# The first warm-up of TensorE: five matmuls of 512 columns instead of eight

## The chip, the core and the metric

The kernel runs on one core of a Trainium2 chip. A core has a matrix engine (TensorE, "PE" in the profile, with its weight loads shown apart as "PEld"), a vector engine (VectorE, "DVE"), a scalar engine (ScalarE, "ACT"), a general engine (GpSimd, "POOL") and a queue engine (SyncE, "SP"). They run side by side and wait for each other through semaphores. The metric is the device time of one execution in microseconds.

## What is computed

The reference is attention with two kinds of heads, followed by a mixture of four experts that all see every token:

```python
# q, k, v: (4 batches, 8 heads, 768 tokens, 64)
scores = scale * q @ k.T
mask   = causal                                  # heads 0, 2, 6
         or causal & (sink of 4 | window of 64)  # heads 1, 3, 4, 5, 7
a   = softmax(where(mask, scores, -1e9))
x   = (a @ v) -> (3072 tokens, 512)
p   = domain_probs / (domain_probs.sum(-1) + 1e-9)   # (3072, 4)
out = sum over e of p[:, e] * (relu(x @ w1[e]) @ w2[e])   # w1: 512 x 1024, w2: 1024 x 512
```

## The kernel before

All instructions of all engines stand in an order written out by hand: each engine runs its own list in the order in which the program issues it, and each waits only where its data do.

The attention is cut into eight blocks (four batches, two halves of 384 tokens). Block 0, `attention(0, 0)`, is issued by itself at the start. The other seven are woven into the experts' matmuls by a plan of costs and due times. The experts' work takes the 24 tiles of 128 tokens in order: tiles 0 to 3 first (`plain_steps`), then pairs of tiles (`pair_steps`).

Only block 0 matters here, because the change stands right before it. Its parts on TensorE come in this order:

- `warm_up(ps_warm, 8, 512)` (called at L1461; the matmul is L446): matmuls of a tile of zeros, `warm`, which VectorE clears first (L431). They write a PSUM bank that nobody reads.
- `transposes(0)` (L574): q and k of heads 0 and 1 are turned by six f32 matmuls against an identity, three for q and three for k. q and k of this block come by their own DMAs, one for each head: eight for k on SP's queue (L409), the first four for q on ACT's queue and four on SP's (L422). The identity is made on POOL (masks.py).
- `scores(0)` (L676, with the mask added by L688). It begins with another `warm_up` of five matmuls of 128 columns (L446), which stands between the transposes and the first real matmul. That matmul waits for VectorE's copy of the keys out of PSUM into `kR` (L593).
- `transposes(1)` (heads 2 and 3), `scores(2)` with a `warm_up` of eight matmuls of 128 columns, then scores and values of the other heads mixed, with small warm-ups of 256 columns at five more places, and `transposes(2)` and `transposes(3)` between them. ScalarE takes the exponentials (L694) and the reciprocals of the sums (L822, L832).
- At the end the result is turned (L781) and scaled (L827) into `xT`, and the first experts' matmuls (L1050) read it, from 21.7 us on.

```python
    def warm_up(ps, n, cols):
        for _ in range(n):
            nc.tensor.matmul(
                out=ps[:, 0:cols], lhsT=warm[:, 0:P], rhs=warm[:, 0:cols],
                start=True, stop=True,
            )
```

Of the kernel before, what the change touches and what calls it, by code (L numbers as in the profile page):

```python
# [19 lines left out]
def kernel(  # L20
# [421 lines left out]
    ps_warm = pO.tile([P, DM], FP32, name="pO", bufs=2)  # L442
# [7 lines that stand above are left out]
# [1008 lines left out]


    nc.vector.memset(x_one[:, :, D:P], 0.0)  # L1460
    warm_up(ps_warm, 8, 512)  # L1461
    for ns in attention(0, 0):
        tick(ns)
    tick(LAG)
# [107 lines left out]
```

## Time and profile before

| what | value |
|---|---|
| median of 5 runs | 377.7 us (377.23 to 378.61) |
| profiled execution | 377.59 us, of which span 375.9 us |
| PE busy | 368.5 us, 98% of the span, 4128 matmuls |
| PEld / DVE / ACT / POOL busy | 83% / 72% / 61% / 30% |
| DMA | 39.24 MB, mean 104 GB/s |
| PE from 21.7 us to the end | 350.25 of 354.20 us busy |

The span is the time from the first to the last instruction of the program in the profiled execution; the device time holds some 1.7 us more around it. All starts below are counted from the span's start. Matmuls are pipelined: the length that the profile gives a matmul includes a tail that overlaps the next one, so the distance between two starts tells what a matmul really takes. "Idle before" in brackets is the time in which an engine had nothing to do before an instruction, with what ended the wait as far as the profile can tell from the semaphores; when an instruction waits for several, the last event before its start is named. The page's second part cuts the span into 40 slices, a digit for each: tenths of busy time, and for PEclk tenths of the full clock that TensorE was granted.

### The profile page before, as it was taken

Reading aid. Unit: us, or ns where it says so; the run is one execution under the profiler, and the core shown is the slowest. Engines: PE = TensorE matmul, PEld = TensorE weight load, DVE = VectorE, ACT = ScalarE, POOL = GpSimd, SP = SyncE. Lnnn points to the kernel's source line nnn. Section 1 sums busy time; section 2 is a strip of 40 time slices with the busy share of each in tenths; the row PEclk is TensorE's granted clock in tenths of the full one; section 3 lists DMA queues with packets and bytes.
Section 4 is the critical chain, followed back from the end, with each engine's and each line's share of the span. In section 5 each row is a group of like instructions: output and inputs, shape, how many; then the busy total and the mean of one; then the engine's idle time right before and its main releaser. Section 6 shows DMA issues by size and latency. Waiting matters only on the chain.

```text
span 375.9 us, 10100 instructions
## 1 busy us (share of the span) xinstructions
PE 368.5 (98%) x4128; PEld 311.2 (83%) x4128; DVE 271.5 (72%) x581; ACT 227.9 (61%) x475; POOL 112.6 (30%) x155
## 2 busy tenths in 40 slices
PE   8899999999999999999999999999999999999996
PEld 5755466668998988999989898998899998999995
DVE  7774768697787669868668858967768858559461
ACT  3863478547785785765776855784777361551630
POOL 8924673854057039115501650320000000000000
PEclk9999999999999999999999999999999999999999
DMA  8999999999699599998904991951220300300101
GB/s 157 157 203 208 192 188 193 172 171 151 103 109 153 91 98 123 159 114 63 198 4 64 170 157 25 126 121 12 72 68 3 114 2 0 114 2 22 37 2 57
DMA packets 123747, 39.24 MB, mean 104 GB/s; under 512 B 113728, under 2 KB 116356, under 8 KB 123700
## 3 DMA queue, kind: packets, MB, share of 16 engines
q0 software_dynamic: 85824, 19.01, 59.8%
q1 hardware_dynamic: 36276, 19.18, 22.9%
q8 instruction: 32, 0.52, 0.6%
q10 hardware_dynamic: 1600, 0.39, 0.5%
q14 instruction: 15, 0.12, 0.1%
HBM read 44.89 MB, written 6.34 MB: 136 GB/s over the span
## 4 chain that ended last, share of the span: by engine, by line
PE 95%; DVE 2%; ACT 2%; issue 0%
PE pO L1315 31%; PE pA L1179 25%; PE pO L1208 9%; PE pA L1050 7%; PE pO L1071 7%; PE pA L676 6%; PE pV L732 2%; PE pV L804 2%; PE pA L1208 2%; PE pO L446 1%; PE pA L574 1%; ACT es L694 1%; DVE xs L1135 1%; PE pA L1405 0%; ACT rc L822 0%; DVE xT L827 0%
## 5 line engine op out<-in xcount | busy, mean ns | idle before, releaser
L1315 PEld LDWEIGHTS <-hA 128*128 128x128 f16 x1104 | 104.9, 98 | 12.3
L1179 PE MATMUL pA<-xs,w1sb 128*128 128x256 f16 x864 | 109.3, 272 | 0.0
L1179 PEld LDWEIGHTS <-w1sb 128*128 128x128 f16 x864 | 80.7, 98 | 8.5
L1188 ACT ACTIVATE hA<-pA 128x512 f16<-128x512 f32 x108 | 64.4, 597 | 35.2 <-PE pA L1179 33.0
L1315 PE MATMUL pO<-w2sb,hA 128*128 128x256 f16 x640 | 76.7, 272 | 0.0
L694 ACT ACTIVATE es<-pA 128x384 f16<-128x384 f32 (+2 forms) x122 | 59.2, 512 | 26.7 <-PE pA L676 22.9
L306 POOL DMA_DIRECT2D vS<-in_v_dram x30 | 29.6, 986 | 110.0 <-PE pV L804 108.2
L1315 PE MATMUL pO<-tsb,hA 128*128 128x256 f16 x464 | 56.7, 272 | 0.0
L1135 DVE TENSOR_TENSOR xs<-xT,pB 128x1024 f16<-128x1024 f16 (+1 forms) x52 | 49.5, 970 | 1.4 <-DMA xT<-x_pair 1.4
L990 DVE TENSOR_TENSOR hA<-hA 128x1024 f16<-128x1024 f16 x60 | 39.7, 685 | 0.4
L1063 ACT ACTIVATE hA<-pA 128x384 f16<-128x384 f32 (+1 forms) x64 | 22.2, 385 | 19.4 <-PE pA L1050 19.2
L1050 PE MATMUL pA<-xT,w1sb 128*128 128x384 f16 (+1 forms) x256 | 31.1, 273 | 0.7 <-DVE xT L827 0.3
L1071 PE MATMUL pO<-w2sb,hA 128*128 128x512 f16 x128 | 30.7, 379 | 0.0
L1335 ACT COPY s<-pO 128x256 f32<-128x256 f32 x31 | 11.5, 372 | 27.7 <-PE pO L1315 21.9
L827 DVE TENSOR_TENSOR xT<-pV,rc 64x384 f16<-64x384 f32 x37 | 20.5, 555 | 10.3 <-ACT rc L832 7.8
L1050 PEld LDWEIGHTS <-w1sb 128*128 128x128 f16 x256 | 19.3, 98 | 9.8 <-issue 1.5
L1208 PEld LDWEIGHTS <-w1sb 128*128 128x128 f16 x416 | 26.3, 98 | 1.1 <-issue 0.2
L1225 DVE CUSTOM_DVE_ANT_0 hA<-pO,s 128x512 f16<-128x512 f32 x26 | 17.7, 689 | 12.5 <-PE pO L1208 8.8
L822 ACT ACTIVATE rc<-pV,eps 64x384 f32<-64x384 f32 x37 | 21.3, 575 | 6.5 <-PE pV L804 5.9
L698 DVE TENSOR_TENSOR es<-es,mS 128x384 f16<-128x384 f16 (+1 forms) x40 | 13.7, 344 | 15.0 <-ACT es L694 15.0
L676 PE MATMUL pA<-qT,kR 128*128 128x384 f16 (+2 forms) x120 | 23.1, 280 | 0.4 <-DVE kR L593 0.2
L1218 ACT COPY s<-pO 128x512 f32<-128x512 f32 x39 | 22.5, 586 | 1.4 <-PE pO L1208 1.2
(144 smaller groups left out, 487.6 us busy)
## 6 DMA issues: line engine op xcount, KB each, us to landing
pB<-p_rows SPq DMA_DIRECT2D x10, 512.0 KB
out_dram<-o SPq DMA_DIRECT2D x19, 256.0 KB
w1sb<-in_moe_w_dram POOLq DMA_DIRECT2D x8, 512.0 KB, 9.2
w2sb<-in_moe_w_dram POOLq DMA_DIRECT2D x4, 1024.0 KB, 12.3
vS<-in_v_dram POOLq DMA_DIRECT2D x30, 112.0 KB, 4.5
k_rows<-in_k_dram POOLq DMA_DIRECT2D x18, 128.0 KB, 5.0
q<-in_q_dram POOLq DMA_DIRECT2D x18, 128.0 KB, 6.9
vR<-in_v_dram POOLq DMA_DIRECT2D x24, 48.0 KB, 5.6
```

The costliest lines, as they stand in the source:

```text
L306: gp.dma_start(out=t[:, :, own_v(h)], in_=windows_of(v, b, h, c))
L676: nc.tensor.matmul(out=ps[:, o : o + nq], lhsT=key_tile(b, c, h, t), rhs=qTs[b, c][:, hp, q0 : q0 + nq], start=(n == 0 or not first), stop ...
L694: nc.scalar.activation(out=es[:, 0:cols], in_=ps[:, 0:cols], func=AF.Exp, scale=SC)
L990: nc.vector.tensor_tensor(out=out, in0=a, in1=b, op=ALU.subtract)
L1050: nc.tensor.matmul(out=pss[ft][:, 0:cols_n], lhsT=w1_tile(e, ct, ft), rhs=x[:, ct, :], start=(n == 0), stop=(n == DMP - 1),)
L1071: nc.tensor.matmul(out=ps_o, lhsT=hs[:, ft, j * P : (j + 1) * P], rhs=w2sb[:, e * FTP + ft, :], start=(ft == 0), stop=(ft == FTP - 1),)
L1135: nc.vector.tensor_tensor(out=o, in0=xin, in1=pb.to_broadcast([P, DMP, n, P]), op=ALU.mult)
L1179: nc.tensor.matmul(out=ps[:, f * PC : (f + 1) * PC], lhsT=w1_tile(e, ct, f0 + f), rhs=xs[:, ct, :], start=(ct == 0), stop=(ct == DMP - 1),)
L1188: nc.scalar.activation(out=blocks[:, b0 : b0 + 2, k0 : k0 + 2, :].rearrange("p t f x -> p f t x"), in_=ps.rearrange("p (f t x) -> p f t x" ...
L1208: nc.tensor.matmul(out=ps[:, f * P : (f + 1) * P], lhsT=w[:, ct, f * P : (f + 1) * P], rhs=a[:, ct, :], start=(first and f == 0 and ct == ...
L1218: nc.scalar.copy(out=kept[n], in_=ps)
L1315: nc.tensor.matmul(out=ps, lhsT=a[:, k, :], rhs=b(k), start=(first and k == 0), stop=(k == KT - 1), skip_group_check=not first,)
```

## The change

The number of matmuls in the first warm-up goes from eight to five. The width of 512 columns, the operands and the place stay.

```diff
     nc.vector.memset(x_one[:, :, D:P], 0.0)
-    warm_up(ps_warm, 8, 512)
+    warm_up(ps_warm, 5, 512)
     for ns in attention(0, 0):
         tick(ns)
     tick(LAG)
```

On TensorE three pairs of weight load and matmul (L446) fall out at the head of the list. The rest of that list, and the lists of the other engines, hold the same instructions in the same order.

## The prediction

> **What bounds the kernel now.** I read the page first: busy shares, granted clock, chain that ended last.
>
> ```profile
> PE 368.5 (98%) x4128; PEld 311.2 (83%) x4128; DVE 271.5 (72%) x581; ACT 227.9 (61%) x475; POOL 112.6 (30%) x155
> ...
> PEclk9999999999999999999999999999999999999999
> ...
> PE 95%; DVE 2%; ACT 2%; issue 0%
> ```
>
> TensorE (PE) is the bound, and no DMA stands in the chain. A microsecond that PE loses at the start comes out at the end, unless some wait after the place of the loss is ended by something that does not move with PE. The slices cannot show the start: 40 slices of 9.4 us are too coarse.
>
> Next, the timeline of PE and of its weight loads (PEld) from 1 to 10 us. Columns: start, length from the first start to the last end, engine and line, shapes, count, and in brackets the idle time before it and what ended it.
>
> ```profile
> 1.27 3.59 PE L446 MATMUL pO<-early 128*128 128x512 f16 x8 [1.27 <-DVE early L431]
> 3.80 0.15 PEld L446 LDWEIGHTS <-early 128*128 128x128 f16 x1 [0.28 <-issue]
> 4.55 1.19 PEld L574 LDWEIGHTS pA<-early,hA 128*128 128x128 f32 x6 [0.59 <-POOL early L466]
> 4.66 1.49 PE L574 MATMUL pA<-early,hA 128*128 128x128 f32 x6
> 5.94 0.74 PE L446 MATMUL pA<-early 128*128 128x128 f16 x5
> 6.79 0.61 PE L676 MATMUL pA<-qT,kR 128*128 128x128 f16 x2
> 7.19 0.32 PE L688 MATMUL pA<-early,ident 128*128 128x256 f16 x1
> 7.34 0.27 PE L676 MATMUL pA<-qT,kR 128*128 128x256 f16 x1
> 7.45 0.22 PE L688 MATMUL pA<-early,ident 128*128 128x128 f16 x1
> 7.51 0.82 PE L574 MATMUL pA<-early,hA 128*128 128x128 f32 x6
> 8.26 0.61 PE L446 MATMUL pA<-early 128*128 128x128 f16 x8
> 8.97 0.11 PEld L676 LDWEIGHTS <-kR 128*128 128x128 f16 x2 [0.29 <-DVE kR L593]
> 8.98 0.39 PE L676 MATMUL pA<-qT,kR 128*128 128x128 f16 x2
> ```
>
> The reader is to see two things. First, where the changed warm-up ends: its eight matmuls run from 1.27 to 4.66, 0.42 us apart, and the six transposes of heads 0 and 1 (L574) come right behind. Their first weight load starts at 4.55, after 0.59 us in which the load path stood idle while the last warm-up matmul was still running. It waited for its operand, so the data of q heads 0 and 1 arrived only then (the releaser named, a POOL mask, is merely the last event before it; POOL's own part, the identity, was written by 1.4 us). Second, the speed: equal work runs at two speeds. Six f32 transposes take (1.49 - 0.42)/5 = 0.21 us apiece at 4.66 and (0.82 - 0.27)/5 = 0.11 at 7.51; 128 columns of f16 take 0.107 at 5.94 and 0.056 at 8.26. So PE runs at half clock first, 0.83 ns a column, and at full clock later, 0.43. The change falls inside the row at 7.19: its 256 columns last until 7.34, 0.15 us, between 0.21 (half) and 0.11 (full). Hence the clock came up at about 7.27, 6.0 us after PE's first matmul, all but one gap of 0.3 us (before 6.79) being work. The granted clock is no help here: it reads 9 in the first slice too, and 1.00 in a window of 1.27 to 4.66, because the profile has no record before the first change.
>
> Last, windows of the stretches behind it: busy time by engine, granted clock, DMA.
>
> ```profile
> 10.68:14.10 3.42, 3.42 (x42) 3.04 (x41) 3.25 (x12) 2.36 (x7) 3.42 (x6) 1.00 1.66 114
> 14.10:21.70 7.60, 5.76 (x61) 4.34 (x60) 5.02 (x12) 6.82 (x15) 5.69 (x11) 1.00 1.07 194
> 21.70:375.90 354.20, 350.25 (x3973) 298.15 (x3972) 255.33 (x537) 214.46 (x446) 94.02 (x118) 1.00 0.82 101
> ```
>
> PE is idle under 4 us of the last 354, so nothing there swallows a shift. Between 14.1 and 21.7 ACT is the busier engine, but the chain enters it from PE (the L804 matmuls at 13.37) and leaves it to PE. A shift passes through.
>
> **The change part by part.** It removes three matmuls with their three weight loads, the last of the first warm-up, and nothing else; all other instructions keep their order on every engine.
>
> 1. *What is taken away.* 3 x 0.427 us = 1.28 us. PE then ends the warm-up at 3.38 instead of 4.66.
> 2. *What starts earlier.* The transposes cannot start before their data. Weight load at 4.55, matmul at once behind it (elsewhere, as at 8.97 and 8.98, the two start together), so 4.55 instead of 4.66: -0.10 us. The other 1.18 us become idle PE. Bounds: 0 if the data are 0.1 us later in another execution, -1.28 if they were there at 3.38; the row says 0.10.
> 3. *What the idle time does to the clock.* PE now works 2.1 us, rests 1.2, and works again from 4.55. The trace shows one rise of the clock only, after 6.0 us of nearly unbroken work, and it stayed up over later gaps, the longest 1.05 us. What a gap of 1.2 us does before the rise, it does not show. Lower bound: nothing, the rise stays at 7.27. Nearest row otherwise: the same 6.0 us, counted anew from 4.55, put it at 10.55. I take the latter: the 2.1 us of work before the gap are less than the 3.4 us of unbroken work (1.27 to 4.66) that left the clock at half in this trace. Upper bound: the breaks of 0.3 us at 6.4 and 8.7 restart it as well, and it comes some 3.5 us later still, at 14.1.
> 4. *What half clock costs from 7.27 to 10.55.* The scores of head 0 start 0.10 earlier, at 6.69, and have 128 + 384 + 256 + 256 + 128 = 1152 columns: 0.96 us at half clock, so the next transposes start at 7.65 instead of 7.51: +0.14. The six transposes then take 1.28 us as at 4.66, instead of 0.65: +0.63. The eight small warm-up matmuls behind them (0.86 instead of 0.45) lie under the VectorE copy of the keys, which holds the next scores until 0.8 us after the transposes, and nearly 0.9 with the longer tail of a transpose at half clock (0.42 instead of 0.27): nothing; without that cover they would cost 0.4. The scores of head 2, at 8.98 before, are again 1152 columns, 0.96 instead of 0.50: +0.46, less 0.08 for what runs after 10.55. Sum: 0.14 + 0.63 + 0.46 - 0.08 = +1.15, the 0.10 of step 2 in it.
> 5. *What is later behind it.* q and k land no later than before, so these loads only get more slack; weight loads on POOL's queue do not wait for PE at that point. All engines shift together.
>
> [...]
>
> I lean slightly below the sum: the medians are of other executions, in which the clock may have come up earlier than 7.27, and one delayed from there costs less. +1.1 us on the profiled execution's 377.59 (span 375.9, and 1.7 around it) gives **378.7**, 1.0 over the median of 377.7.
>
> **The rivals.** About 0.2% (0.76 us) is what a measurement of this kernel can tell from no change.
>
> [...]
> - *The clock misses another round* (slower). To the 1.15 comes half clock from 10.68 to 14.1, where PE is busy all of 3.42 us: at most +1.7 and at least half of that, so 379.6 to 380.4; I take 380.0. For it: breaks of 0.3 us remain. Against it: at half clock the work between the breaks is twice as long.
> - *The warm-up stood in the way* (faster). In runs without the profiler the q heads 0 and 1 may land sooner. Each 0.1 us sooner than 4.55 is 0.1 us that the eight matmuls hold up and the five don't, down to 3.38. It decides if the data come before 3.9 and the clock rises where it did: then over 0.76 us is gained, at 3.4 up to 1.28, 376.3. For it: these are the first transfers of all, and 3.7 us from issue to use (0.81 to 4.55) is long. Against it: the row at 4.55, and a profiled time equal to the others.
>
> **How the numbers follow.** Forecast 0.62, own range 378.1 to 379.3; no effect on the clock 0.20; another round 0.09; faster 0.09. Of the forecast some 0.06 fall under 0.76 us, where the count is nearer to the shorter one. So slower 0.56 + 0.09 = 0.65, same 0.20 + 0.06 = 0.26, faster 0.09. The range leaves out the faster case below and the upper half of the other round above: 377.4 to 379.9.
>
> **What would show it.** In the timeline after: the L446 row with five matmuls ending near 3.4; PE idle about 1.2 us; L574 at 4.55. At 7.5 to 7.7 the second set of transposes either 0.21 apart (forecast) or 0.11 (no effect on the clock), and the first matmuls at 0.056 for 128 columns near 10.5. The first L1050 pair of matmuls, at 21.68 before, about 1.1 later, and from there equal stretches. The prediction is wrong if the clock comes up at the same time, if it takes until the experts' matmuls, or if something fixed in time, a weight transfer, holds PE at 20 to 22 us.

## The result

The changed kernel takes 378.63 us (median of 26 runs, 377.98 to 379.86) against 377.68 (44 runs, 377.23 to 378.62): 0.95 us more. The two medians stand as 1.0025 to 1; the ratio estimated from all runs is 1.0023, with a 95% interval of 1.0017 to 1.0028. The forecast was 378.7.

The profiled execution of the changed kernel has a span of 377.4 us, 1.5 over that of before, more than the medians differ. Its first 10 us, in the timeline of PE (columns as before):

```profile
1.27 2.31 PE L446 MATMUL pO<-early 128*128 128x512 f16 x5 [1.27 <-DVE early L431]
4.66 1.51 PE L574 MATMUL pA<-early,hA 128*128 128x128 f32 x6 [1.08 <-DMA hA<-in_q_dram]
5.97 0.74 PE L446 MATMUL pA<-early 128*128 128x128 f16 x5
6.82 0.61 PE L676 MATMUL pA<-qT,kR 128*128 128x128 f16 x2
7.22 0.42 PE L688 MATMUL pA<-early,ident 128*128 128x256 f16 x1
7.43 0.39 PE L676 MATMUL pA<-qT,kR 128*128 128x256 f16 x1
7.65 0.24 PE L688 MATMUL pA<-early,ident 128*128 128x128 f16 x1
7.72 0.82 PE L574 MATMUL pA<-early,hA 128*128 128x128 f32 x6
```

The wait of PE now stands in the row: 1.08 us until a q transfer lands. The transposes start at 4.66 all the same, because their data came later here. Half clock lasts a little longer: the 256 columns at 7.22 and at 7.43 take 0.21 and 0.22 us (half clock), the 128 at 7.65 take 0.07, between half (0.107) and full (0.056), and the transposes at 7.72 run at full clock, (0.82 - 0.27)/5 = 0.11 us apart. The trace's clock record begins at 7.67 us, against 7.27 in the profile of before. So the clock rose only 0.4 us later in this execution, and all that PE has lost when the chain reaches the experts is 0.31 us (L781 at 20.41 instead of 20.10). The other 1.15 us come later. The same timeline from 20 to 49 us, first before, then after (three dots stand for rows left out, here and below):

```profile
20.10 0.34 PE L781 MATMUL pV<-ident,x_pair 128*128 128x128 f16 x3
...
21.68 0.48 PE L1050 MATMUL pA<-xT,w1sb 128*128 128x384 f16 x2 [0.27 <-DVE xT L827]
...
33.38 0.36 PE L577 MATMUL pV<-ident,q 128*64 128x128 f16 x6
...
47.34 0.81 PE L1050 MATMUL pA<-xT,w1sb 128*128 128x384 f16 x4
```

```profile
20.41 0.34 PE L781 MATMUL pV<-ident,x_pair 128*128 128x128 f16 x3
21.54 4.77 PE L1050 MATMUL pA<-xT,w1sb 128*128 128x384 f16 x26 [0.79 <-DMA w1sb<-in_moe_w_dram]
...
34.08 0.36 PE L577 MATMUL pV<-ident,q 128*64 128x128 f16 x6 [0.32 <-DMA q<-in_q_dram]
...
48.81 0.81 PE L1050 MATMUL pA<-xT,w1sb 128*128 128x384 f16 x4 [0.60 <-DMA w1sb<-in_moe_w_dram]
```

PE waits three times for a transfer. The first wait costs nothing by the third L1050 matmul (at 21.99, inside the second row), which had to wait for `xT` anyway: it is again 0.31 us behind before. The second adds 0.39 us and the third 0.76, which makes 1.46.

The three waits hang together. POOL issues the next loads of k and q only after it has read a mark out of the first w1sb tiles (L519). That row, before and after:

```profile
20.48 0.18 POOL L519 COPY seen<-w1sb 1x1 f16<-1x1 f16 x1 [1.80 <-DMA w1sb<-in_moe_w_dram]
```

```profile
21.46 0.18 POOL L519 COPY seen<-w1sb 1x1 f16<-1x1 f16 x1 [2.80 <-DMA w1sb<-in_moe_w_dram]
```

The load itself was issued at the same time (L335, 11.93 and 11.91), so its landing was 1 us later. POOL's list hands this on: the next k and q loads, the mark out of q (34.16 instead of 33.21) and the next w1sb loads (38.31 instead of 37.36) all come 0.95 to 0.98 us later, and these w1sb loads took another 1.2 us longer to land (mark at 48.79 instead of 46.64). So the chain that ended last, on the page, is another one than before:

```profile
PE 85%; DMA 8%; POOL 4%; DVE 1%; issue 0%; POOLq 0%
```

One profile therefore does not explain the median: 0.31 us of it is the clock, and 1.15 are waits for loads whose instructions the change does not touch. What the two causes are worth on the whole had to come from more traces.

### The profile page after: what moved, and what is told of

Its sections match the earlier page's. It is cut to its first block, busy times and chain, and to the rows that moved or that the text cites. A ratio compares the mean times of both kernels' runs of the same rounds, so it can differ in the third digit from the quotient of the medians.

```text
span 377.4 us, 10094 instructions
## 1 busy us (share of the span) xinstructions
PE 367.7 (97%) x4125; PEld 310.8 (82%) x4125; DVE 271.7 (72%) x581; ACT 227.9 (60%) x475; POOL 113.1 (30%) x155
## 4 chain that ended last, share of the span: by engine, by line
PE 85%; DMA 8%; POOL 4%; DVE 1%; issue 0%; POOLq 0%
PE pO L1315 31%; PE pA L1179 25%; PE pO L1208 9%; DMA w1sb<-in_moe_w_dram 5%; PE pA L1050 5%; PE pA L676 5%; PE pO L1071 5%; DMA q<-in_q_dram 3%; PE pV L732 2%; PE pV L804 2%; PE pA L1208 2%; POOL vR L304 1%; POOL vS L310 1%; DVE xs L1135 1%; PE pA L1405 0%
## 5 line engine op out<-in xcount | busy, mean ns | idle before, releaser
L1063 ACT ACTIVATE hA<-pA 128x384 f16<-128x384 f32 (+1 forms) x64 | 22.2, 385 | 20.5 <-PE pA L1050 20.3
L1050 PE MATMUL pA<-xT,w1sb 128*128 128x384 f16 (+1 forms) x256 | 30.9, 273 | 1.5 <-DMA w1sb<-in_moe_w_dram 1.4
L1050 PEld LDWEIGHTS <-w1sb 128*128 128x128 f16 x256 | 19.3, 98 | 10.5 <-issue 2.3
L1208 PEld LDWEIGHTS <-w1sb 128*128 128x128 f16 x416 | 26.3, 98 | 1.1 <-issue 0.2
L822 ACT ACTIVATE rc<-pV,eps 64x384 f32<-64x384 f32 x37 | 21.3, 575 | 6.5 <-PE pV L804 5.9
```

What stands on the lines that cost most here:

```text
L1050: nc.tensor.matmul(out=pss[ft][:, 0:cols_n], lhsT=w1_tile(e, ct, ft), rhs=x[:, ct, :], start=(n == 0), stop=(n == DMP - 1),)
L1208: nc.tensor.matmul(out=ps[:, f * P : (f + 1) * P], lhsT=w[:, ct, f * P : (f + 1) * P], rhs=a[:, ct, :], start=(first and f == 0 and ct == ...
```

## The experiments

Three theories. *Theory 1, the hole:* the clock rises at the end of a stretch in which PE worked most of the time; the idle 1.2 us spoil every stretch that holds them, so that none costs the same as five. How long such a stretch is and how much of it may be idle, no trace shows; the ranges that the expectations give by it for the rise are the author's estimates. *Theory 2, each matmul counts:* the less work before, the later the clock, in proportion. *Theory 3, the weight load:* the difference is the later landing of w1sb, seen in the profile above. All kernels below are the kernel before with another line L1461, but for one, and compute the same; the clock's rise is the start of the trace's clock record.

### None, two, five, six, seven, eight

```diff
-    warm_up(ps_warm, 8, 512)
+    pass
```

> No first warm-up at all; PE's first work is the six transposes at about 4.6 us. [...] So none costs the same as five: 378.6 us (378.3 to 378.9), ratio 1.0023 to before, the clock up between 7.5 and 11 us. Theory 2 (each matmul counts): three fewer cost 0.95 us, eight fewer then cost about 2.5 us, 380.2, the clock up at 11 us or later. Theory 3 (the weight load): the difference comes from the w1sb transfer, which landed at 21.4 instead of 20.4 us in the profile of the changed kernel; the number of matmuls matters only through it; in this run w1sb lands at 21.4 us or later and PE waits for it.

```diff
-    warm_up(ps_warm, 8, 512)
+    warm_up(ps_warm, 6, 512)
```

> Six matmuls; the warm-up ends at 3.80 us and PE idles 0.75 us before the transposes. [...] Theory 2: two thirds of the loss of five, 378.3 us. Theory 3: w1sb lands as late as with five, 378.6 us.

```diff
-    warm_up(ps_warm, 8, 512)
+    warm_up(ps_warm, 7, 512)
```

> Seven matmuls; the warm-up ends at 4.23 us, idle 0.3 us. Theory 1: as before, 377.5 to 377.8 us, the 0.1 us that the transposes start earlier included. Theory 2: a third of the loss, 378.0 us. Theory 3: 378.6 us if any shorter warm-up shifts the weight load, 377.7 if not.

The changed kernel again, `warm_up(ps_warm, 5, 512)`:

> The changed kernel again (five), for a second trace and for a time beside the others: 378.6 us, ratio 1.0023. Theory 1: the clock rises between 7.5 and 11 us, at another moment than the 7.67 of the first profile, and the start of L781 x3 (20.41 in the first profile, 20.10 before) moves with it, by up to 1.3 us. Theory 3: w1sb lands at about 21.4 again and the first L1050 matmul waits for it, whenever the clock rises.

and a third time, for one more trace:

> The changed kernel a third time, for a third trace. Theory 1: the clock rises between 7.5 and 11 us and the start of L781 x3 lies 0.3 to 1.3 us after the 20.10 of before, the later the later the clock. Theory 3: PE waits for w1sb at 21 us and again at 34 and 48 us, as in the first profile of the changed kernel (in its second trace it did not).

The kernel before for a second trace:

> The kernel before again, for a second trace. Theory 1: the clock rises between 3.9 and 7.3 us, at another moment than 7.27; below 7.27, L781 x3 starts before 20.10, down to 19.7. Where PE is that early, the first L1050 matmul waits for w1sb, which landed between 20.4 and 21.5 us in the traces so far. Theory 3: w1sb lands near 20.4 with eight matmuls, and not later.

and against itself with repeated timing:

> The kernel before against itself: how far two equal kernels differ by this measurement. Every theory: ratio 1.0000, inside 0.9990 to 1.0010; an interval that leaves out 1 here would mean that differences of 0.1% in the other runs say nothing. Theory 1: the clock rises between 3.9 and 7.3 us.

Two matmuls:

```diff
-    warm_up(ps_warm, 8, 512)
+    warm_up(ps_warm, 2, 512)
```

> Two matmuls of 512 columns, PE idle from 2.1 to about 4.6 us. Theory 1: as with none and with five, the clock between 7.5 and 11 us and 378.3 to 378.6 us, ratio 1.0013 to 1.0025. Each matmul counting for itself: between none and five cannot be told apart by theory 2 any more, since none (378.58) and five (378.36) already differ by no more than their scatter; a time near 377.8 or above 379 would contradict theory 1.

Measured. "Third L1050" is the start of the third experts' matmul, where PE leaves the first block of attention behind; with it the first 22 us can be compared free of what follows. Ratios stand to runs of the kernel before on the same chip.

| first warm-up | run | median us | ratio, 95% interval | clock rises at us | third L1050 at us |
|---|---|---|---|---|---|
| 8 | profile before | 377.68 (44 runs) | | 7.27 | 21.68 |
| 8 | w8b | 377.25 (one run) | | 5.22 | 21.24 |
| 8 | w8c | 377.73 | 1.0009, 1.0001 to 1.0018 | 6.73 | 21.64 |
| 7 | w7 | 377.69 | 0.9991, 0.9980 to 1.0002 | 5.35 | 21.53 |
| 6 | w6 | 378.27 | 0.9993, 0.9971 to 1.0016 | 8.62 | 22.39 |
| 5 | profile after | 378.63 (26 runs) | 1.0023, 1.0017 to 1.0028 | 7.67 | 21.99 |
| 5 | w5 | 378.36 | 1.0015, 1.0003 to 1.0027 | 9.78 | 22.39 |
| 5 | w5c | 378.16 (one run) | | 7.92 | 22.18 |
| 2 | w2 | 378.45 | 1.0021, 1.0011 to 1.0030 | 7.91 | 22.20 |
| 0 | w0 | 378.58 | 1.0014, 1.0002 to 1.0026 | 7.93 | 22.19 |

The null run, w8c, comes out at 1.0009 with an interval that leaves out 1, so a difference of 0.1% between two of the short series says nothing by itself, as its expectation put it. The times alone would not carry much beyond the main comparison; together with the clock they agree. None costs what five costs, and theory 2 falls: it asked 380.2 us for none, and got 378.58. From eight to seven nothing is lost. Six lies at the edge: four of its twelve times are 377.44 to 377.62, as most with eight, and the other eight 378.24 to 378.89, as with five. Eight has some of the longer times too: 13 of its 44 lie at 378.0 or above. Of the 38 with five in the two series none lies below 377.9. Six's ratio of 0.9993 is no proof of the contrary: its median is 0.45 us over the 377.82 of the runs of before beside it, one of these took 382.72, and the interval is wide.

The rows that the reader should put side by side are the six transposes of heads 0 and 1, and of heads 2 and 3. Timeline of PE with none (w0):

```profile
4.76 1.51 PE L574 MATMUL pA<-early,hA 128*128 128x128 f32 x6 [4.76 <-DMA hA<-in_q_dram]
...
7.75 0.31 PE L688 MATMUL pA<-early,ident 128*128 128x128 f16 x1
7.85 0.86 PE L574 MATMUL pA<-early,hA 128*128 128x128 f32 x6
```

Five, in the run where the clock came late (w5):

```profile
4.45 1.51 PE L574 MATMUL pA<-early,hA 128*128 128x128 f32 x6 [0.87 <-DMA hA<-in_q_dram]
...
7.43 0.31 PE L688 MATMUL pA<-early,ident 128*128 128x128 f16 x1
7.54 1.49 PE L574 MATMUL pA<-early,hA 128*128 128x128 f32 x6
8.82 1.06 PE L446 MATMUL pA<-early 128*128 128x128 f16 x8
9.67 0.44 PE L676 MATMUL pA<-qT,kR 128*128 128x128 f16 x2
```

Eight, in the run where it came early (w8b):

```profile
4.74 1.07 PE L574 MATMUL pA<-early,hA 128*128 128x128 f32 x6
...
6.96 0.89 PE L574 MATMUL pA<-early,hA 128*128 128x128 f32 x6
...
8.57 0.38 PE L676 MATMUL pA<-qT,kR 128*128 128x128 f16 x2
```

Six transposes span 1.5 us at half clock and 0.8 to 0.9 at full clock. With five in w5 both sets are slow, and the scores of head 2 start at 9.67; with eight in w8b the clock rises inside the first set, and they start at 8.57. The same program with five (w5, w5c, the profile after) gets its clock at 9.78, 7.92 and 7.67, so the moment is not fixed by the program alone. Still, the traces fall in two groups, late5 below aside, whose work begins 1.4 us later: where the warm-up left a hole of 0.85 us or more before the transposes (w6, the three with five, w2, w0) the rise came at 7.67 to 9.78, and where it left 0.5 or less (the three with eight, w7, and the three traces of the filled kernels below) at 4.92 to 7.27.

Theory 1 can be checked by where the rise lies in each trace. A length of unbroken work alone does not give it: in the profile before PE worked without a break from 1.27 to 6.47, and the clock stayed at half until 7.27, while in w8b, the same program, it rose at 5.22. In the three traces with eight PE's first matmul starts at 1.27, and the clock rose 3.95, 5.46 and 6.00 us later.

From the end of the last 0.427 us to the first transpose, seven matmuls left a gap of 0.49 us in the trace, six 0.85, five 1.29, 1.08 and 1.46 (the rows say 0.2 less, since they count the last matmul's tail). With a gap of 0.49 or none the rise came 3.65 us (fill256) to 6.00 us (profile before) after PE's first matmul. With 0.85 or more it came 6.40 us (profile after) to 8.51 us (w5) after it. Counted from the first transpose instead, these rises lie at:

| first warm-up | run | first transpose at us | clock rises, us after it |
|---|---|---|---|
| 6 | w6 | 4.66 | 3.96 |
| 5 | profile after, w5, w5c | 4.66, 4.45, 4.84 | 3.01, 5.33, 3.08 |
| 2 | w2 | 4.69 | 3.22 |
| 0 | w0 | 4.76 | 3.17 |

With none the transposes are PE's first work, and the clock rose 3.17 us after their start; with two, five and six it rose 3.01 to 5.33 us after it. So in these traces the work ahead of a gap of 0.85 us or more brought the rise no more than 0.16 us nearer, and in three of five no nearer at all. To that extent theory 1 holds where the kernels differ. Two things limit it. Between 0.49 and 0.85 us no gap was measured, and six and seven have one trace each. And how long the stretch is, and what share of it must be work, is not shown; I had put the clock of six about as early as with eight, and in its trace it rose at 8.62.

Theory 3 falls in its strong form: w1sb was on time for five in w5 (the first L1050 at 20.98, no wait for a transfer) and late with seven in w7:

```profile
19.86 0.34 PE L781 MATMUL pV<-ident,x_pair 128*128 128x128 f16 x3
21.20 1.46 PE L1050 MATMUL pA<-xT,w1sb 128*128 128x384 f16 x8 [1.00 <-DMA w1sb<-in_moe_w_dram]
```

With seven PE was ahead of before by 0.24 us at L781, and stood 1.00 us for w1sb. At the third L1050 it was ahead by 0.15. The load sets a floor under executions with an early clock, and it scatters: PE got it at 20.3 us in w8b and 21.5 in w0. The waits at 34 and 48 us of the profile after did not return in w5 (none) and in w5c (0.15 us at 39.0, at the first matmul that reads the next w2sb).

A weaker form stays open. POOL's mark out of the first w1sb came at 20.26, 20.48 and 20.59 us with eight and at 20.9, 21.3 and 21.46 with five, so later in each trace; w2 (20.36) speaks against a rule, w0 (21.42) for it. No run here moves the load alone.

### The same five, later

```diff
-    nc.vector.memset(warm.bitcast(FP32), 0.0)
 ...
-    one_values(nc.vector, 0)
+    one_values_r(nc.vector, 0, 0)
+    x = vS[:, 0, :, :, :]
+    fill(nc.vector, x[0:R0, :, :, :].rearrange("p t s x -> p (t s x)"), ONES)
+    nc.vector.memset(warm.bitcast(FP32), 0.0)
+    fill(nc.vector, x[:, :, 0:2, D:P], ONES)
+    fill(nc.vector, x[:, :, 2:5, 0:D], ONES)
 ...
-    warm_up(ps_warm, 8, 512)
+    warm_up(ps_warm, 5, 512)
```

> Five matmuls of 512 columns, but their tile is cleared 1.3 us later, so they run from about 2.6 to 4.75 us without a gap before the transposes (which start up to 0.2 us later than with five). Same work as the changed kernel; the idle time lies before the work and not within it. Theory 1: the first good stretch can begin at about 2.1 us, so the clock rises between 5.5 and 9 us: between the two kernels, 378.0 to 378.3 us, the 0.2 us of delay included. Amount of work alone: as the changed kernel, 378.4 to 378.6 us. An unbroken run into the transposes alone: as before, 377.7 to 377.9.

Measured: 378.13 us, ratio 1.0015 (1.0005 to 1.0025); PE works from 2.69 without a gap into the transposes at 4.79; the clock rises at 8.54, inside the forecast 5.5 to 9, and the third L1050 starts at 22.47. Counted from PE's first matmul the rise came after 5.85 us, within the 3.95 to 6.00 of the traces with eight. The time is what theory 1 named, 378.0 to 378.3; but it is only some 0.2 us from what the changed kernel gives in its short series, so the time does not decide here. Against the reading that an unbroken run into the transposes is enough speaks the trace: its clock rose at 8.54, later than in any trace with eight (7.27 at the latest).

### Filling the gap with smaller matmuls

```diff
-    warm_up(ps_warm, 8, 512)
+    warm_up(ps_warm, 5, 512); warm_up(ps_warm, 11, P)
```

> Five matmuls of 512 columns, then eleven of 128 (0.107 us each at half clock, 1.17 us), so PE works until about 4.55 us as with eight, but in smaller pieces, and 16 matmuls in all. [...] If it were the five matmuls of 512 columns themselves, or the number of rows of zeros, and not the gap, the time stays at 378.4 (ratio 1.0015 to 1.0028). Theory 3 (weight load): no different from five.

The same kernel again:

> Five matmuls of 512 and eleven of 128 again. In the first trace the clock rose at 6.47 us and PE was 0.21 us ahead of before at 21.5, but it waited 0.37 us for w2sb at 38.7 and a little for VectorE at 248, and the eleven times had a median of 378.33. If those waits are the transfers' own scatter: 377.5 to 378.0 this time, ratio to the kernel before near 1. If this kernel brings them about (its list on TensorE is eight matmuls longer): again about 378.3 with PE waiting for w2sb near 38.7. Theory 1 holds only for the stretch up to 21.5 us either way: the clock rises between 3.9 and 7.3.

```diff
-    warm_up(ps_warm, 8, 512)
+    warm_up(ps_warm, 5, 512); warm_up(ps_warm, 6, 256)
```

> Five matmuls of 512 columns and six of 256: the same 3.41 us of work from 1.27 to 4.68 us as eight of 512, in eleven pieces. Theory 1: the clock rises between 3.9 and 7.3 us, and the time is that of before, 377.5 to 378.0, ratio 0.9995 to 1.0010. If filling with more, smaller matmuls costs something later on, as the first fill run suggests: 378.1 to 378.4. If only the width of 512 columns counted for the clock: 378.4, the clock after 7.5.

| filled with | run | median us | ratio, 95% interval | clock rises at us | third L1050 at us | end against before, from there |
|---|---|---|---|---|---|---|
| 11 of 128 | fill | 378.33 | 1.0016, 1.0006 to 1.0025 | 6.47 | 21.47 | +0.81 |
| 11 of 128 | fillb | 378.32 | 1.0014, 1.0005 to 1.0022 | 7.19 | 21.66 | +0.66 |
| 6 of 256 | fill256 | 377.82 | 1.0002, 0.9993 to 1.0011 | 4.92 | 21.26 | +0.41 |

The last column is the shift of PE against the profile of before, at the last matmuls less that at the third L1050. Up to 22 us all three do what theory 1 says: the clock is early (4.92 to 7.19), and PE is level with before or ahead. fill256 has the time of before. Eleven matmuls of 128 twice gave 378.3, where theory 1 asked for the time of before; that is near the 378.4 expected if the gap did not count, but with a clock that rose early. Their loss lies far behind. In fill256 and fill PE first waits for w2sb at 38.4 and 38.7 us and loses 0.41 and 0.54 there; that takes back what the early clock had gained, and in fill more. Then, in both runs with eleven, comes a wait at 248 us that no other trace has. VectorE's wait in the profile before, then VectorE from 243 to 248 us in fillb, then the L1208 matmuls of PE that wait for it there:

```profile
245.19 1.29 DVE L1135 TENSOR_TENSOR xs<-xT,pB 128x512 f16<-128x512 f16 x2 [1.42 <-DMA xT<-x_pair]
```

```profile
243.07 0.69 DVE L1225 CUSTOM_DVE_ANT_0 hA<-pA,s 128x512 f16<-128x512 f32 x1
246.64 1.29 DVE L1135 TENSOR_TENSOR xs<-xT,pB 128x512 f16<-128x512 f16 x2 [2.88 <-DMA xT<-x_pair]
247.85 0.28 DVE L990 TENSOR_TENSOR xs<-xs,kS 128x256 f16<-128x256 f16 x1
```

```profile
248.20 0.62 PE L1208 MATMUL pO<-xs,w1sb 128*128 128x128 f16 x8 [0.49 <-DVE xs L990]
```

The transfer that turns `x_pair` was issued at 241.87 us on SP's queue, as before (241.81), but VectorE got `xT` at 246.64; in the profile of before it was 245.19, after an idle time of 1.42 us. PE loses 0.66 us there, and 0.27 in fill. Why this transfer takes 1.4 us longer with eight more matmuls in TensorE's list, and not with three more in fill256, stays open; no run settled it. So the times show the cost of the gap less cleanly than the clock does: fill256 and w7, with a short gap or none, have the time of before; the kernel with eleven has not, because of a wait that lies elsewhere.

## Why the prediction was right, step by step

- *Chain and bound.* Right for the shift on PE's path: where no transfer interferes (w0, w5, w2, w6), PE stays behind by the same 0.5 to 0.7 us from the third L1050 to the end. But "no DMA stands in the chain" held for that one execution only. The expert weights arrive close to when PE needs them: PE stood 0.25 (fill256), 0.34 (w8b), 0.79 (profile after) and 1.00 us (w7) for the first w1sb, and not at all in the profile before and in w5. And they scatter by one microsecond (20.3 to 21.5 us). They cut short what an early clock gains (w7, fill256), and added 1.15 us to the profile after. The prediction gave the whole loss to the clock and had no term for them.
- *Step 1, what is taken away.* As forecast: the fifth matmul ends near 3.38 us, and the rest is idle.
- *Step 2, earlier start, -0.10.* The mechanism is right, the transposes start when their data land; the size is lost in scatter. They started at 4.66, 4.45 and 4.84 with five, and with eight in w8b at 4.74, later than the warm-up's end.
- *Step 3, the clock.* Right that the idle time delays the rise. Wrong in its rule: the 6.0 us of work "counted anew" from 4.55 gave 10.55, and the rises were 7.67, 7.92 and 9.78. They lie 3.01 to 5.33 us after the first transpose. I took the 6.0 us of one profile for a length of work; the other two traces with eight show 3.95 and 5.46. With five, none of the three rises came as late as forecast. The 3.5 us that the upper bound adds are an estimate that no run shows: the latest rise was at 9.78, not at 14.1.
- *Step 4, the price.* The path was right: in w5, where the second transposes ran at half clock throughout, the scores of head 2 start at 9.67 instead of 8.98, 0.69 later, where the sum's first two terms made 0.77. But it was sized for a rise at 10.55 against one at 7.27: +1.15. The traces give less for less: against the third L1050 of the profile before, +0.31 for a rise at 7.67, +0.50 for 7.92 and +0.70 for 9.78. But before had mostly risen earlier than its profile showed (5.22, 6.73 and 7.27; third L1050 at 21.52 us on the mean, against 22.19 with five, 0.67 apart). Both errors have the same source and opposite signs, and the sum of 1.0 over the median came out near the 0.95 measured. That it came so near is luck. On the mean of three traces a side PE's last matmul starts 1.1 us later with five: 0.67 of it is there at the third L1050, and about 0.4 are waits for loads behind it, nearly all in one trace. Whether these belong to five matmuls or to chance three traces cannot tell; the second series of five, w5, came out only some 0.6 us (1.0015) over before.
- *Step 5, what is later behind it.* Right that the loads do not wait for PE; I did not see that they were almost late themselves.
- *The rivals.* That the idle time has no effect on the clock (chance 0.20) is out: three traces with five rose at 7.67 or later, three with eight at 7.27 or sooner, and the time moved. "Another round" was not met in a trace (latest rise 9.78). "The warm-up stood in the way" is out: the q data let the transposes start at 4.45 at the soonest in the traces, its condition was before 3.9, and the unprofiled runs were slower too.
- *The chances.* The 0.06 of the forecast that lean on a shorter count have no run behind them: no run shows such a count. What the runs showed with five is a third L1050 0.31, 0.50 and 0.70 us later than in the profile of before, and 0.95 us between the medians.

## What to carry to other kernels

A warm-up must not only be long enough, it must leave no hole: here 0.5 us of idle time before the first real work cost nothing (w7, 377.69 us), 0.85 us cost something in some executions (w6, 378.27), and from 1.1 us on the whole warm-up was as good as none (378.36 in w5, 378.58 with none). Size it to reach to where the first data land: eight to seven matmuls changed nothing, eight to five cost 0.95 us, a quarter of a percent. Before a clock's rise in one profile is made a rule, look at a second profile of the same program.

## What was not expected of the hardware

- The moment of the rise: 5.22, 6.73 and 7.27 us in three traces of the kernel with eight, 7.67, 7.92 and 9.78 in three with five, though PE's first matmul starts at 1.27 in all six. 5.20 us of unbroken work (1.27 to 6.47, profile before) left the clock at half until 7.27, where w8b had it up 3.95 us after the first matmul.
- The f32 transposes: in w0 they are PE's first work, from 4.76 us on, and the clock rose 3.17 us after their start, only 1.86 us after the first f16 matmul (6.07). No run shows by itself whether they count for the clock as f16 matmuls do.
- Loads scatter by a microsecond between executions of nearly the same program (the first w1sb was ready for PE between 20.3 and 21.5 us), and POOL's list hands the delay of one load on to the loads behind it (0.95 to 0.98 us in the profile after).
- Eleven small matmuls at 3.4 us went along, in two traces of two, with a transfer at 242 us that took 1.4 us longer. It is shown, and not explained.
